# Sums of weight blocks made by ScalarE copies and accumulating transfers instead of VectorE additions, with a new order of the first three steps

## The chip, the cores and the metric

The kernel runs on one core of one Trainium2 chip. A core has a matrix engine (TensorE, PE in the profile, with its weight loads shown as PEld), an element-wise engine for tensor operations (VectorE, DVE), one for activations and copies (ScalarE, ACT), a general engine (GpSimd, POOL) and a fifth one that issues transfers (SyncE, SP). Each engine works through its own list of instructions in order and waits on semaphores for the others. Transfers are carried out by 16 DMA engines and are issued from SP, ACT or POOL. The metric is the time of one execution on the device in microseconds (us); less is better. All times below are in us.

## The reference

The computation is a gated linear attention followed by a two-layer network. Everything is in 32-bit floating point on the chip, with batch 4, 8 heads, 768 tokens and head dimension 48.

```python
f = 1.0 / (1.0 + np.exp(-f_logit))
for t in range(S):
    state = f[:, :, t, :, None] * state + np.einsum('bhd,bhe->bhde', k[:, :, t], v[:, :, t])
    y[:, :, t] = np.einsum('bhd,bhde->bhe', q[:, :, t], state)
x = y.transpose(0, 2, 1, 3).reshape(B * S, H * D)          # 3072 x 384
h = x @ w_in                                               # 384 x 2048
g = np.maximum(h, 0.0) + alpha * np.minimum(h, 0.0)
out = g @ w_out                                            # 2048 x 384
```

The weights w_in and w_out arrive as 64-bit numbers and are turned into 32-bit ones on the chip.

## The kernel before

**Steps.** The 768 tokens of a sequence are cut into 6 chunks of 128, and the 4 batches into 2 pairs. A step is one chunk of one pair, so there are 12 steps (0 to 11, even steps for the first pair, odd ones for the second) of 256 tokens each. In every step the attention of a chunk runs first, then the network on its 256 tokens; the attention of the next steps is woven between the network products of the present one.

**The attention of a step.** The gates f, queries q and keys k are loaded with the head dimension on the partitions (`loaded`, L311 to L323; from SP in step 0, from POOL in all others). ScalarE takes the sigmoid of f (L329) and prepares copies (L330, L331); VectorE builds products of neighbouring gates (`lagged_all`, L338 to L345), running sums (`scanned_all`, L373, L374) and the scaled queries and keys (L380 to L406; in the opening steps also `near`, L641). TensorE makes the score products raw (L582), qu (L591, and L681 in the opening steps) and off (L566, blocks off the diagonal). VectorE copies the scores under masks into `ad` (L599, L451, L702), ScalarE places them in the score matrix A (L606, L573, L688). TensorE multiplies A with the values and the old state (py, L614), ScalarE copies that out as y (L494, L729). For the state, the keys are turned: by TensorE (pk, L713) in the opening steps 0 and 1, through two transfers by DRAM (`turned`, `ksn`) in all others; TensorE multiplies them with the values (pd, L539), VectorE and ScalarE update the state (L550, L554, L556).

**The way into the network.** y has the head dimension on its partitions; the network wants all 384 features of a token there. In step 0 TensorE does this with a placing product (xt, L738) and ScalarE copies the result to xT (L747). In step 1 and in the last step four transfers do it (`by_token`, L626, xT<-y), in the others transfers by DRAM (L503, L505, xT<-tokens).

**The network.** The first layer is eight groups of products (`whole`, L831, tile ph), each with 256 columns of w_in (a "piece" of w_in). ScalarE writes relu(-h) (L854), VectorE combines it with h and alpha (L859), which gives the tile gate. From step 3 on, four of the eight pieces (3 to 6) are split in a high and a low part, with reduced-precision products of hi by xh, lo by xl and a third pass of the sums hi + lo with xs (L831 each time). xl and xs of each step are made by a ScalarE copy and an accumulating transfer from POOL (L820, L823). The parts of w_in are made once: hi by ScalarE (`high_of_w_in`, word Y, L770), lo and the sum by two VectorE operations (`rest_of_w_in`, word Z, L774 and L775). Three sums lie at first in the places of xh, xl and xs; before step 3 the network word T (`turnover`, L796) moves and scales them to their own place, which becomes free when the early tiles are closed.

The second layer of step 0 is plain (po, L866, 32 products of 128 x 384). From step 1 on it is done by a scheme of seven block products of half width (`product`, L886: pa, pc, pb, pa, pd, pe, pf) in place of eight. For it w_out is taken as four blocks b11, b12, b21, b22, and four combinations of them are needed: t3 = b22 - b12, t2 = t3 + b11, t4 = t2 - b21 and t1, the difference of b12 and b11, which replaces b12. In before these are eight VectorE operations (`sum_of_w_out`, words W0 to W7, L809, two halves for each). The gate blocks get four similar sums in every step (L880, words Nm, Nu, Nv, Nw), and the block products are combined at the end of each step (L896, words Nd to Nl).

**The weights' loading.** SP loads 8 pieces of each weight as raw 64-bit words (`load_weights`, L277) into five buffers. For each piece ScalarE makes two passes (L281, L282: words a0 to a7 for w_in, b0 to b7 for w_out), and VectorE adds the two results up (L291: words w0 to w7 for w_in, v0 to v7 for w_out).

**The order.** `ORDER_WORDS` is a list of some two thousand words, written out. `0r1` is part r1 of step 0, `3Na2` is network group a2 of step 3, `W3` is one of the words without a step. Each word calls one part of the program, which issues all its instructions for all engines. A manual schedule keeps this order on PE, DVE and ACT; on POOL and SP a scheduler places the transfers.

**Idle products.** Before the first data arrive, and in gaps of steps 0 and 1, TensorE executes products of ones into an unused bank (`idled`, L935): IDLE = 14 at the start, the words I0 to I5 (BEFORE = 6) up to off of step 0, and J0 to J7 (BEHIND = 8) after it. Their results are not used.

Of the kernel before, what the change touches and what calls it, by code (L numbers as in the profile page):

```python
# [27 lines left out]
IDLE, BEFORE, BEHIND = 14, 6, 8  # L28
# [18 lines left out]
0Np5 W0 1Y1 1X W1 Y3 W2 0Np6 W3 2G 1Na0 W4 W5 0Np7 0No0 2h 1M 0No1 2i 1Nr0 1Na1 Y4 Y5 1Na3 2p 1Nr1 2q W6 1Na2 1Na4
Y6 3e 1Nr2 2u0 2l 1Nc0 1Nr3 2t 1Nc1 2k 1Nm0 1Nr4 1Nc2 2r0 1Nc3 W7 1Nm1 1Na5 1Nc4 1Na6 1Nr5 2R0 1Nr6 2r1 2U0 2K Z3
2u1 1Nc6 2R1 2A0 1Na7 1Nr7 1Nc5 2o 1Np0 2U1 2O 3f 1Nc7 2d Z4 1Nk 2D 2A1 1Np2 3F 1Np1 2y0 2y1 1Np3 2Y0 2Y1 2X 1Nu0
1Nu1 1Nv0 3G 3g 1Np4 1Nd 1Nv1 1Nw0 1Ng 2M 1Nw1 1Ne 1Nj 1Nh 1Np5 3h 1Np6 1Nf 1Nl 3p 1Ni 3i 1NL 2Na0 3l 4e 2Nr0 2Na1  # L50
2Nr1 2Na3 2Na2 1Ns1 3q 2Nr2 3r0 3u0 2Nc0 2Nr3 3k 3t 2Nc1 2Nm0 3R0 3U0 2Na5 2Nc2 2Nc3 2Nm1 2Na4 Z5 2Nr4 3r1 2Nr5 3K
3u1 2Na7 3R1 2Na6 3o 3A0 2Nc5 2Nr6 2Nc4 3O 3U1 2Nc6 Z6 3A1 3d 3D 2Np0 2Nr7 2Np1 2Nk 2Nc7 4f 2Nd T 3y0 3y1 4F 3Y0
2Np2 1Ns0 3Y1 3M 4g 2Np3 4r0 2Nu1 2Nu0 2Np4 3X 2Nv0 4G 2Nv1 2Nw0 2Ng 3Nx 3Ny 2Nw1 2Ne 2Nj 2Nh 2Np5 4h 2Np6 2Nf 2Nl
4p 3Na1 3Nz 3Na0 4i 3Nr0 2NL 2Ni 4k 4l 3NY 3Na2 4q 3Nr1 3Na7 4K 3Na3 5e 2Ns1 3Nr2 3Nc0 3NZ 3Na4 3Nc2 4t 3Nc1 3Nr7
3Nm0 4u0 3Nc7 4R0 4U0 3Nq3 3Na6 4r1 4A0 4R1 3Na5 4u1 4U1 3Nq4 3Nq5 3Nq6 4o 4O 3Nb3 3Nr3 3Nc3 3Nb4 3Nm1 2Ns0 3Nb6
3Nb5 4d 3Nr4 3Nr5 4D 3Np0 4A1 3Nr6 3Nc6 3Nc5 4y0 3Nc4 4y1 3Np2 5f 4M 4Y0 4Y1 3Np1 3Nk 5F 4X 5g 3Np3 3Nu0 3Nu1 3Nv0
5G 3Nv1 3Nw0 3Ng 3Np4 4Nx 4Ny 3Nw1 3Nd 3Ne 5h 3Nj 3Np5 3Np6 3Nh 3Nf 3Nl 5p 3Ni 5r0 4Nz 4Na0 5i 4Nr0 4Na1 3NL 5k 4NY
4Na5 5l 4Nq5 4Na2 5q 4Nr1 5K 4Na3 4Nc0 4Nr2 5u0 5t 4Nc1 4Nm0 4Nc2 5R0 5U0 4Na7 4Nr7 4NZ 4Na4 6e 3Ns1 5r1 4Nc7 4Nq4
4Nq3 5A0 5u1 5R1 5U1 4Na6 4Nb5 4Nb3 5o 4Nq6 4Nr3 5d 5O 4Nc3 4Nb4 5A1 4Nm1 5D 4Nr4 4Nr5 4Nb6 4Np0 4Nr6 5y0 4Nc4 4Nc5
6f 4Nc6 5y1 5Y0 6F 4Np2 5Y1 5X 6g 4Nk 4Np1 4Np3 4Nu0 4Nu1 4Nv0 4Nv1 4Ng 6G 5Nx 5M 4Nw0 4Np4 5Ny 4Nw1 4Nd 3Ns0 4Ne 6h  # L60
4Nj 4Nh 4Np5 4Nf 4Nl 6p 4Ni 5Nz 5Na0 4Np6 6i 5NY 6k 5Nr0 5Na1 4NL 6l 5Na2 6q 5Na7 5Nr1 6t 5Nc1 6u0 5Nr2 5Nc0 6r0
5Nm0 5Nc2 6R0 5Nr7 5NZ 7e 4Ns1 5Na4 6K 5Na3 6U0 5Nc7 5Na5 6r1 5Nq3 6A0 6u1 6R1 6U1 5Nq4 5Nb3 5Nq5 5Na6 5Nb4 6o 5Nr3
5Nq6 5Nc3 6O 6A1 6d 5Nm1 5Nb6 6D 5Nb5 5Nr4 5Nr5 5Np0 5Nr6 5Nc4 5Nc6 7f 6y0 5Nc5 5Nk 7F 6y1 6Y0 5Np2 6Y1 5Np1 6X 7g
5Np3 5Nu0 5Ng 7G 5Nu1 5Nv0 5Nv1 5Nw1 5Np4 6Nx 5Nw0 5Nd 6M 5Ne 6Ny 7h 5Nj 5Nh 5Np5 5Nf 5Np6 4Ns0 7p 5Ni 6Nz 6Na0 5Nl
7i 7l 6NY 6Nr0 6Na1 5NL 7k 7q 6Na2 6Nr1 7t 6Nc1 6Nr2 6Nc0 6Na7 6Nm0 7K 6Na3 6Nq3 7r0 6Nc2 7u0 7R0 6Nr7 6NZ 6Na4 8e
5Ns1 7U0 6Nc7 6Nq4 6Na5 7u1 7r1 6Nq5 7A0 7R1 7U1 6Na6 6Nq6 6Nb3 6Nr3 6Nc3 6Nb4 6Nm1 6Nb6 6Nb5 7A1 7o 6Nr4 6Nr5 6Nc4
6Nr6 7d 8f 6Np0 7O 6Nc5 7D 6Nk 6Np1 7y0 8F 7y1 6Nc6 7Y0 6Np2 7Y1 7X 8g 7Nx 7M 6Np3 6Nu0 6Nu1 6Np4 6Nv0 6Nd 6Nv1 6Nw0
6Ng 8G 7Ny 6Ne 6Nj 6Nw1 8h 6Nh 6Np5 6Nf 7NY 6Np6 5Ns0 6Nl 8p 6Ni 8i 7Nz 7Na0 7Nr0 7Na1 7Nr1 6NL 8k 8l 7Na2 8t 8r0
7Nr2 7Nc0 8q 7Nc1 8R0 9e 6Ns1 8K 7Na3 7Nm0 7Na7 8u0 7Nc2 7Nr7 7NZ 7Na4 8U0 7Na5 7Nq3 7Nq4 7Nc7 8r1 8u1 7Nq5 8A0 7Na6
8R1 7Nb4 7Nb3 8U1 7Nq6 7Nr3 7Nc3 7Nm1 7Nb6 7Nb5 8o 8A1 8d 7Nr4 7Nr5 7Nc4 7Nr6 8D 8O 9f 7Np0 7Nc5 7Nk 7Np1 7Nc6 8y0  # L70
9F 8y1 8Y0 8Y1 7Np2 8X 9g 7Nd 8M 7Np3 7Nu0 7Nu1 8Nx 7Ne 7Np4 7Nv1 7Ng 9G 8Ny 7Nv0 7Nw0 7Nw1 7Np5 7Nh 9h 7Nf 7Nj 9r0
7Np6 6Ns0 7Nl 9p 7Ni 9R0 8Nz 8Na0 8Na7 9i 8Nr0 8Na1 7NL 9k 9l 8Na2 9q 8Nr1 8NY 8Nr2 9t 8Nc0 8Nc2 8Nc1 8Nr7 8NZ 8Na4
10e 7Ns1 8Nm0 9u0 9U0 9K 8Na3 8Na5 8Nq4 9A0 8Nq3 9u1 9r1 8Na6 8Nc7 9R1 9U1 8Nq5 8Nq6 8Nb3 8Nb4 8Nr3 8Nc3 8Nm1 8Nb6
8Nb5 8Nr5 9o 8Nr4 8Nc5 9A1 8Nr6 9O 9d 8Np0 8Nc4 9D 8Nk 8Np1 8Nc6 10f 9y0 9y1 8Np2 10F 9Y0 9Y1 9X 10g 9M 8Np3 8Nu0
8Nu1 10r0 8Np4 8Nd 9Nx 8Nv0 8Nv1 8Nw0 8Ng 10G 8Np5 8Ne 8Nw1 9Nz 10h 9Ny 8Nh 8Nj 8Nf 10p 8Np6 7Ns0 8Nl 8Ni 9NY 9Na0
# [25 lines left out]
def kernel(  # L101
# [845 lines left out]
    with tc.manual_schedule(engines={mybir.EngineType.PE, mybir.EngineType.DVE, mybir.EngineType.Activation}):  # L947
# [10 lines left out]
        for key in ORDER:  # L958
            run[key]()
# [55 lines left out]
```

## Time and profile before

| What | us |
|---|---|
| Time, median of 3 runs | 595.74 |
| lowest and highest of them | 594.69, 597.52 |
| Span of the profiled execution (no other time is given for it) | 592.1 |
| Busy in that span: PE | 580.1 |
| PEld | 527.9 |
| DVE | 505.7 |
| ACT | 300.4 |
| POOL | 68.4 |
| First network product (ph of step 0) starts at | 42.70 |

The time of a run is taken from outside the program, the span from the first to the last event of the profiled execution. The profile gives for each engine its busy time, for slices of the span the share that was busy and the clock granted to TensorE (PEclk, 1.00 is full speed), for each wait who ended it, and for each group of instructions its line, its operation, the shape of its tiles and the mean duration. "A<-B" means that an instruction writes tile A and reads tile B. Where an engine's idle time is given "<-issue", nothing that the profile shows had to be waited for.

The row `0.00:42.70` of the stages below is the opening (the loads and the attention of step 0), `42.70:91.00` is the network of step 0 with the attention of step 1, `91.00:141.00` and `141.00:209.00` hold the networks of steps 1 and 2, and from there on the steps repeat in the same form.

### The profile page before, as it was taken

The numbers are of one execution on the slowest core, as the hardware profiler recorded it, in microseconds if no ns is written. First come the engines' busy times: TensorE is split into PE (matmuls) and PEld (weight loads), VectorE is DVE, ScalarE is ACT, GpSimd is POOL, SyncE is SP. The second block draws the span as 40 slices with busy tenths as digits, with TensorE's granted clock in tenths as the row PEclk, the third lists the DMA queues.
The fourth block names the chain that finished last, engine by engine and source line by source line (L and its number), as shares of the span: only waits on it lengthen the run. The fifth ranks groups of instructions, "written<-read, shape, count | busy, mean of one in ns | idle before, by whom it ended". The sixth has DMA issues, their size and how long they took to land.

```text
span 592.1 us, 18853 instructions
## 1 busy us (share of the span) xinstructions
PE 580.1 (98%) x8200; PEld 527.9 (89%) x8200; DVE 505.7 (85%) x1027; ACT 300.4 (51%) x561; POOL 68.4 (12%) x114
## 2 busy tenths in 40 slices
PE   8799999999999999999999999999999999999997
PEld 6678767899899999999999999899899999899997
DVE  7889799899999989899989889989989979966243
ACT  5697973461472473483382374374275355443230
POOL 9110010000101101111111101101100100100100
PEclk9689999999999999999999999999999999999999
DMA  9959212612523823724624614722732731611300
GB/s 299 356 160 348 98 22 63 172 30 86 123 86 91 191 78 89 172 65 105 169 60 106 153 68 106 164 74 85 148 110 81 152 110 54 112 44 30 80 2 27
DMA packets 69443, 67.57 MB, mean 114 GB/s; under 512 B 44688, under 2 KB 58640, under 8 KB 69360
## 3 DMA queue, kind: packets, MB, share of 16 engines
q1 hardware_dynamic: 59744, 37.16, 22.1%
q0 software_dynamic: 8880, 28.84, 19.2%
q8 instruction: 64, 1.05, 0.7%
q10 hardware_dynamic: 736, 0.37, 0.2%
q14 instruction: 19, 0.16, 0.1%
HBM read 44.99 MB, written 13.50 MB: 99 GB/s over the span
## 4 chain that ended last, share of the span: by engine, by line
PE 80%; issue 10%; DMA 4%; ACT 3%; DVE 3%; POOL 1%; POOLq 0%; ACTq 0%; DVEq 0%
PE ph L831 36%; PE pa L886 9%; PE pd L886 5%; PE pf L886 5%; PE pe L886 5%; PE pb L886 5%; PE pc L886 4%; PE py L614 3%; PE qu L591 3%; PE raw L582 3%; DMA w_out_raw<-in_w_out 2%; PE pd L539 1%; PE off L566 1%; DVE ad L451 1%; DMA f<-in_fT 1%
## 5 line engine op out<-in xcount | busy, mean ns | idle before, releaser
L831 PE MATMUL ph<-xT,w_in_sb 128*128 128x256 f32 x612 | 137.1, 380 | 0.2 <-DMA xT<-y 0.2
L831 PEld LDWEIGHTS ph<-xT,w_in_sb 128*128 128x128 f32 x612 | 115.1, 190 | 16.9 <-issue 0.9
L854 ACT ACTIVATE gate<-ph 128x512 f32<-128x512 f32 x96 | 54.6, 594 | 134.4 <-PE ph L831 127.5
L859 DVE SCALAR_TENSOR_TENSOR gate<-gate,om,ph 128x256 f32<-128x256 f32 x192 | 81.0, 476 | 25.6 <-ACT gate L854 25.1
L886 PE MATMUL pa<-w_out_sb,gate 128*128 128x192 f32 x352 | 61.7, 329 | 0.0
L880 DVE TENSOR_TENSOR gate<-gate 128x512 f32<-128x512 f32 x88 | 57.6, 690 | 3.2 <-PE pb L886 2.4
L886 PEld LDWEIGHTS pa<-w_out_sb,gate 128*128 128x128 f32 x352 | 57.1, 190 | 0.5
L599 DVE COPY_PREDICATED ad<-mraw,raw 128x256 f32<-128x256 int32 (+1 forms) x96 | 42.7, 445 | 8.9 <-PE raw L582 6.2
L451 DVE COPY_PREDICATED ad<-mquad,qu 128x224 f32<-128x224 int32 (+6 forms) x140 | 42.2, 302 | 6.8 <-PE qu L591 1.7
L606 ACT COPY A<-ad 32x256 f32<-32x256 f32 x96 | 38.7, 403 | 11.8 <-DVE ad L451 10.4
L440 DVE TENSOR_TENSOR scores<-scores,fs 128x768 f32<-128x768 f32 (+5 forms) x60 | 37.4, 623 | 1.6
L844 ACT ACTIVATE ph<-ph 128x512 f32<-128x512 f32 x36 | 20.2, 574 | 34.0 <-PE ph L831 25.2
L831 PE MATMUL ph<-xh,hi 128*128 128x256 f32 x216 | 34.4, 295 | 0.0
L831 PE MATMUL ph<-xl,lo 128*128 128x256 f32 x216 | 32.0, 283 | 0.3 <-issue 0.3
L886 PE MATMUL pb<-t,gate 128*128 128x192 f32 x176 | 31.2, 331 | 0.0
L831 PEld LDWEIGHTS ph<-xh,hi 128*128 128x128 f32 x216 | 28.7, 190 | 2.8 <-issue 1.6
L424 ACT COPY A<-q 48x512 f32<-48x512 f32 x44 | 27.2, 617 | 7.8 <-DVE q L398 7.2
L886 PE MATMUL pd<-t,gate 128*128 128x192 f32 x176 | 30.7, 328 | 0.3 <-DVE gate L880 0.3
L886 PE MATMUL pc<-t,gate 128*128 128x192 f32 x176 | 30.6, 327 | 0.0
L886 PE MATMUL pf<-w_out_sb,gate 128*128 128x192 f32 x176 | 30.5, 327 | 0.0
L323 POOL DMA_DIRECT2D vs<-in_v x22 | 13.2, 605 | 149.4 <-PE py L614 149.1
L886 PE MATMUL pe<-w_out_sb,gate 128*128 128x192 f32 x176 | 30.4, 326 | 0.0
(153 smaller groups left out, 1044.0 us busy)
## 6 DMA issues: line engine op xcount, KB each, us to landing
w_out_raw<-in_w_out SPq DMA_DIRECT2D x8, 767.8 KB, 9.6
w_in_raw<-in_w_in SPq DMA_DIRECT2D x8, 767.2 KB, 9.5
q<-in_qT POOLq DMA_DIRECT2D x11, 512.0 KB, 5.1
f<-in_fT POOLq DMA_DIRECT2D x11, 512.0 KB, 5.2
k<-in_kT POOLq DMA_DIRECT2D x11, 512.0 KB, 4.2
turned<-f SPq DMA_DIRECT2D x40, 128.0 KB, 4.4
ksn<-turned SPq DMA_DIRECT2D x10, 512.0 KB, 3.5
out<-o SPq DMA_DIRECT2D x24, 192.0 KB, 1.9
```

What stands on the lines that cost most here:

```text
L424: nc.scalar.copy(A[halves(cc)[1], :, par * HP:(par + 1) * HP, CH * cc:CH * (cc + 1)], x["q3"][rows(par)].rearrange("p (u h c) s t -> p u h ...
L440: nc.vector.tensor_tensor(by_four(us[:, :, UO[m]:UO[m] + 4 * n]), by_four(us[:, :, skip:skip + 4 * n]), spread(fq[:, :, 1:1 + n], n), ALU. ...
L451: nc.vector.copy_predicated(ad[:, u, :, :, 4 * m:DB], mquad[:, lo:lo + n].bitcast(I32).unsqueeze(1).unsqueeze(1).broadcast_to((128, 2, HP, ...
L582: nc.tensor.matmul(raw[DB * j:DB * (j + 1), par, hp * C:hp * C + QW], lhsT=x["k"][r_, g * DB:(g + 1) * DB], rhs=qd[r_, g], start=True, sto ...
L599: nc.vector.copy_predicated(adu[:, :, :, d:4], mraw[:, d, :, d:4].bitcast(I32).unsqueeze(1).broadcast_to((128, H, NB, n)), rv[:, :, QO[d]: ...
L606: nc.scalar.copy(A[s_, u, :, s_], ad[s_, u].rearrange("p r h t -> p (r h) t"))
L831: nc.tensor.matmul(banks[f][:, j * T:(j + 1) * T], lhsT=of[:, kt, 128 * j:128 * (j + 1)], rhs=by[:, kt], start=first_ and kt + j == 0, sto ...
L844: nc.scalar.activation(banks[f], banks[f], AF.Copy, scale=1.0 - 1.0 / EPS)
L854: nc.scalar.activation(to, of, AF.Relu, scale=-1.0)
L859: nc.vector.scalar_tensor_tensor(to[:, j], to[:, j], om[:, m:m + 1], of[:, j], ALU.mult, ALU.add)
L880: nc.vector.tensor_tensor(block(to)[:, p], block(x_)[:, p], block(y_)[:, p], op)
L886: nc.tensor.matmul(banks[to][:, 0:DH], lhsT=block(of)[:, f], rhs=of_w_out(by)[:, f], start=start and f == 0, stop=f == NH - 1, skip_group_ ...
```

## The change

There are four edits.

1. **W: combinations of w_out.** Each of the eight words is now a ScalarE copy of one block (with sign) into the target, then a transfer from POOL that adds the other block to it. t3 = -b12 and then + b22; t2 = b11 + t3; t4 = -b21 + t2; t1 now has the other sign, b11 - b12, so the combinations that use pe (parts f and l of a step's output) have the scale -UP.
2. **Z: parts of w_in.** Each of the four words is a ScalarE copy hi/EPS into lo, a transfer that adds the piece of w_in to it, a ScalarE copy -hi into the sum, and a transfer that adds lo to it.
3. **The words are cut.** A part is now a generator, and a word in the order is one instruction (or a short run of them); a word that stands several times in `ORDER_WORDS` is carried on each time. The loads of a step are four words (ef, eq, ek, ev) in place of one. The manual schedule now covers POOL and SP also, so that their order is written out as well. The tiles that a part makes are made when first needed (`Later`, `ahead`).
4. **The order.** In steps 0 to 2 the order is new on all engines; from step 3 on the order on each engine is that of before, except for the place of the f and q loads on POOL (f, q, k in place of q, f, k where they stand together). BEFORE is 12 in place of 6: six more idle products, I6 to I11.

In numbers of instructions issued: TensorE has 6 more (4434 to 4440), VectorE 16 fewer (1029 to 1013), ScalarE 16 more (573 to 589), POOL 16 more transfers (119 to 135, 384 KB each), SP the same 132. On SP the opening is now f, q, k of step 0, five pieces of w_in (6, 0, 2, 4, 3), the first values, then w_out piece 1 among the rest of w_in, and the other pieces of w_out.

```diff
-IDLE, BEFORE, BEHIND = 14, 6, 8
+IDLE, BEFORE, BEHIND = 14, 12, 8
...
-0e 1e 0I0 0f 0F 0G 0g 0r1 0h 0i 0m 0p 0j 0r0 0I1 0l 0I2 a0 0R0 0I3 0I4 0I5 0q 0o a1 0k a2 0O 0s 0t w0 0u0 0U0 0R1
...
+0ef 0f 0F 0eq 0f 0f 0F 0F 0F 0F 0g 0g 0g 0g 0ek 0F 0g 0I0 0r1 0r0 0I1 a6 0i 0g 0G a0 1ef a2 a0 0G a4 0R0 0h 0j a3 0m
+0R0 0s 1eq 0p 0I2 a6 0I3 0p 0p 0p 0R0 0q a2 a2 0I4 0I5 0R0 0I6 a6 0p 0I7 0s 0I8 a4 0ev 0q 0l 0l 0I9 0I10 0ev a0 0t 0t
+0I11 0o 0O 0O 0u0 0O 0U0 0U0 0U0 0O 0R1 0H0 0H0 0H0 0R1 b1 0k 0K0 0R1 0R1 0K1 0A0 1f w2 0J0 0J1 0A0 0J2 1ek 0H0 0u1
...
+class Later(dict):
+
+    def __init__(self):
+        self.make = {}
+
+    def __missing__(self, key):
+        self[key] = self.make[key]()
+        return self[key]
+
+
+class Word:
+
+    def __init__(self, part):
+        self.part, self.left = part, None
+
+    def __call__(self):
+        if self.left is None:
+            got = self.part()
+            self.left = got if hasattr(got, "gi_frame") else iter(())
+        next(self.left, None)
...
+        def f_():
+            x["kt"] = load("f", fT)
+            x["f"] = quads(x["kt"])
+
+        def q_():
+            x["q"] = load("q", qT)
...
+        return {"ef": f_, "eq": q_, "ek": k_, "ev": v_}
...
+    def added(to, of):
+        nc.gpsimd.dma_start(out=to, in_=of, accum_op=ALU.add)
+
     def rest_of_w_in(f):
-        w, hi = piece_of_w_in(f), late["hi"][:, f - SPLIT[0]].bitcast(F32)
-        nc.vector.scalar_tensor_tensor(late["lo"][:, f - SPLIT[0]], hi, 1.0 / EPS, w, ALU.mult, ALU.add)
-        nc.vector.scalar_tensor_tensor(sums[f - SPLIT[0]], hi, 1.0 / EPS - 1.0, w, ALU.mult, ALU.add)
+        hi, lo = (late[n][:, f - SPLIT[0]] for n in ("hi", "lo"))
+        nc.scalar.activation(lo, hi.bitcast(F32), AF.Copy, scale=1.0 / EPS)
+        yield
+        added(lo.bitcast(F32), piece_of_w_in(f))
+        yield
+        nc.scalar.activation(sums[f - SPLIT[0]], hi.bitcast(F32), AF.Copy, scale=-1.0)
+        yield
+        added(sums[f - SPLIT[0]].bitcast(F32), lo.bitcast(F32))
...
     def sum_of_w_out(n):
-        to, x_, y_, op = (("t3", b22, b12, ALU.subtract), ("t2", "t3", b11, ALU.add), ("t4", "t2", b21, ALU.subtract),
-                          ("t1", b12, b11, ALU.subtract))[n // 2]
+        to, of, sign, more = (("t3", b12, -1.0, b22), ("t2", b11, 1.0, "t3"), ("t4", b21, -1.0, "t2"), (b12, b12, -1.0, b11))[n // 2]
         p = slice(n % 2 * NH // 2, (n % 2 + 1) * NH // 2)
-        to, x_, y_ = (of_w_out(t) if isinstance(t, str) else t for t in (to, x_, y_))
-        nc.vector.tensor_tensor(to[:, p], x_[:, p], y_[:, p], op)
+        to, more = (late[t] if isinstance(t, str) else t for t in (to, more))
+        nc.scalar.activation(to[:, p], of[:, p], AF.Copy, scale=sign)
+        yield
+        added(to[:, p], more[:, p])
...
             if by_parts(f):
                 products(f, late["hi"][:, f - SPLIT[0]], late["xh"], True, False)
+                yield
                 products(f, late["lo"][:, f - SPLIT[0]], late["xl"], False, False)
...
-            f=lambda: plus(side("11"), "pe", side("11")),
+            f=lambda: plus(side("11"), "pe", side("11"), -UP),
...
-            l=lambda: plus(side("01"), "pe", side("01")),
+            l=lambda: plus(side("01"), "pe", side("01"), -UP),
...
-    with tc.manual_schedule(engines={mybir.EngineType.PE, mybir.EngineType.DVE, mybir.EngineType.Activation}):
+    with tc.manual_schedule(engines={mybir.EngineType.PE, mybir.EngineType.DVE, mybir.EngineType.Activation,
+                                     mybir.EngineType.Pool, mybir.EngineType.SP}):
...
+        run = {key: Word(part) for key, part in run.items()}
         for key in ORDER:
             run[key]()
```

More of the change, by code (lines that the diff above doesn't have):

```diff
@@ L47 @@
[L47 to L51, printed above, removed]
@@ L597, in lags @@
         for d in range(4):
+            if d:
+                yield
             n = 4 - d
@@ L633, in opening @@
         i = f"{bp}_{c}"
+        ahead(bp, c, x)
         def two(name):
```

260 lines of the change are left out of this document (171 added, 89 removed).

## The prediction

> **What bounds the kernel now.** I read the page's busy shares, the slices and the chain first, then the five stages, TensorE's waits, the microseconds in which its clock fell, its rows in time, and what the moved work costs. All times are us.
>
> ```profile
> PE 580.1 (98%) x8200; PEld 527.9 (89%) x8200; DVE 505.7 (85%) x1027; ACT 300.4 (51%) x561; POOL 68.4 (12%) x114
> PEclk9689999999999999999999999999999999999999
> PE 80%; issue 10%; DMA 4%; ACT 3%; DVE 3%; POOL 1%; POOLq 0%; ACTq 0%; DVEq 0%
> ```
> ```profile
> 0.00:42.70 42.70, 35.84 (x696) 29.00 (x697) 34.10 (x62) 30.81 (x59) 17.88 (x45) 0.84 0.84 279
> 42.70:91.00 48.30, 48.11 (x518) 36.27 (x513) 44.13 (x76) 39.68 (x69) 3.67 (x6) 1.00 0.44 157
> 91.00:141.00 50.00, 49.95 (x666) 44.32 (x667) 46.15 (x92) 21.40 (x41) 3.40 (x5) 1.00 0.31 86
> 141.00:209.00 68.00, 67.31 (x1054) 60.89 (x1054) 64.13 (x136) 31.97 (x59) 7.43 (x10) 1.00 0.47 118
> 209.00:592.10 383.10, 378.92 (x5297) 357.40 (x5282) 317.16 (x665) 176.58 (x334) 35.97 (x48) 1.00 0.38 93
> ```
> Columns of the stages: window, length, busy time of PE, PEld, DVE, ACT and POOL, TensorE's granted clock, DMA share, GB/s. From 42.70, the first network product, TensorE is busy to within 0.2 a stage (141 to 209: 0.7). Only the first 42.70 hold time that can be won: what TensorE does there is partly filler, and the clock averages 0.84.
>
> ```profile
> PE off_0a L566 <- DVE kh L402: 2.8, 1, 2.8
> PE py L614 <- ACT ad L688: 0.8, 1, 0.8
> PE off L566 <- issue: 0.7, 1, 0.7
> PE pd L886 <- DVE gate L880: 0.3, 1, 0.3
> ```
> ```profile
> 18.00:19.00 1.00, 0.46 (x28) 0.38 (x15) 0.98 (x3) 0.68 (x3) 0.00 (x0) 0.97 1.06 395
> 19.00:20.00 1.00, 1.00 (x7) 1.00 (x6) 0.92 (x3) 0.58 (x2) 0.00 (x0) 0.50 1.02 381
> 32.00:33.00 1.00, 1.00 (x4) 0.80 (x4) 1.00 (x3) 0.96 (x3) 0.00 (x0) 0.70 0.82 328
> ```
> ```profile
> 12.22 2.43 PE L935 MATMUL idle<-ones 128*128 128x256 f32 x10
> 17.47 0.21 PE L566 MATMUL off_0a<-q,kh 48*32 48x32 f32 x1 [2.83 <-DVE kh L402]
> ...
> 42.70 3.50 PE L831 MATMUL ph<-xT,w_in_sb 128*128 128x256 f32 x15
> ```
> The last filler ends at 14.65, TensorE waits 2.83, does small products, and its clock halves at about 19 until 32.6: qu (L591, L681) takes 1.05+1.97 a half where it takes 0.82+1.11 at full clock (65.37, 66.12). After 42.70 VectorE costs TensorE 0.3, so taking work off VectorE (44.13 busy of 48.30) saves by itself almost nothing.
>
> **The change, part by part.**
>
> *VectorE's relief.* Eight W additions (L809, 0.95 each, 0.87 apart) between 79.3 and 107.6 and eight Z (L774, L775, the same) between 113.5 and 168.6 go: 16 x 0.87 = 13.9. Their cover is TensorE, so I enter 0; the bounds are 0 and the 0.3 wait.
>
> *ScalarE's copies.* 16 more copies of 128x768. Nearest row: hi (L770), 0.84, 13.4 in all. ScalarE is busy 21.40 of 50 from 91 to 141, so 0 beside TensorE; without that room, the gates queued behind each copy would be 0.84 late.
>
> *Accumulating transfers.* 16 of 384 KB on POOL. The nearest rows are the same transfer for x:
>
> ```profile
> xl<-xT POOLq DMA_DIRECT2D x9, 384.0 KB, 4.0
> xs<-xl POOLq DMA_DIRECT2D x9, 384.0 KB, 4.0
> f<-in_fT POOLq DMA_DIRECT2D x11, 512.0 KB, 5.2
> w_out_raw<-in_w_out SPq DMA_DIRECT2D x8, 767.8 KB, 9.6
> ```
> They land in 3.9 to 5.6 and cost POOL about 0.9 to issue (16 x 0.9 = 14.4 of a queue busy 12%). The sums are a chain: t3, then t2 from t3, then t4 from t2, each a copy (0.84) and a landing (4.0). A Z is likewise copy, transfer, copy, transfer. Walked in the new order (each instruction after its producers and its queue, with the durations here), t3 is issued at 80.1 and 95.7 (the second behind a load on POOL), t2 lands by 108.6, t4 by 113.5; pb, the first that reads t4, starts about 122.8. The slack of 9 hides it: cost 0. Uncovered, three links at 5.6 instead of 4.0 would add 4.8, still inside. The Z sums land about 165; their reader T (L796) comes about 172. [...]
>
> *The opening's order and six fillers.* A filler is two records, and ten took 2.43, so one is 0.49 at most. Eleven now stand before off, from about 12.2, and end at 17.1 to 17.5. They cost nothing: off (0.69) and then qu follow, and qu waits for VectorE's running products (near, L641) until 19.2 in any case; if VectorE were 1 earlier, they would hold TensorE up by nothing still. Its longest pause falls from 2.83 to under 1.9, so I take the clock to stay full. Then, in the new order: qu of half 0 19.2 to 21.2; pk 1.04, to 22.4; fillers; qu of half 1 23.8 to 25.7; its masked copies (L702, three, 0.91) end 26.65, before 30.24. ScalarE, whose weight passes (0.80 each) are packed earlier, places the blocks by 31.85; y of half 0 32.4, py of half 1 34.0 to 35.1, xt to 37.2, xT copies 38.2. VectorE's two last weight pieces (L291, 0.94) are ready at 38.2 and 39.1, raw of the next step ends 38.9. The first ph starts at 38.9 instead of 42.70: **+3.8**. On the queues: POOL loads f before k and q instead of q first, and SP puts five w_in pieces ahead of v and w_out; the DMA share is 1.0 until 32 either way, so this only chooses which piece is late, and the walk has each at its place in line. If the clock halves all the same, 4.3 after the last filler as before (at 21.5), qu of half 1 ends 28.5 and all is 2.0 to 2.8 later: +1.0 to +1.8. [...]
>
> *From 39 to 91.* Products stay back to back where weights and gates allow; the nearest misses are ph3 (needs VectorE at 47.2, starts 49.3) and ph1 (52.8, 53.6). One load suffers: w_out piece 4 is issued on SP only after ScalarE has freed its buffer at about 60.6, and ScalarE reads it at 66.25. The eight w_out loads took 6.8 to 15.0; off the opening's crowd the 6.8 is nearest, and ScalarE stalls 1.2 with y of the step behind it. So 60.6 + 6.8 - 66.25 = 1.2; the bounds are 0 (buffer free earlier) and 3.9 (9.6). I enter **-1.2**.
>
> *Step 1's network start.* In before, ph waits 0.19 for xT at 90.91 and its first group lasts 3.14 for 2.60. The raw products of step 2 (two of 0.85) now stand in front and cover it: 0.19 + 0.5 = **+0.7**; bounds 0 and 0.7.
>
> *f of step 3.* Its load (L313, POOL) is now issued behind the transposes of step 2, near 95, lands near 100.1 (5.2), and its sigmoid stands at the head of ScalarE's queue from about 98.2 with two gates behind. In before it was issued at 110.03 and read at 120.55. TensorE has 0.9 of slack at that point; I find it short by 0.9 at the sixth ph and take **-0.5**; bounds 0 and -0.9.
>
> *208.* The 0.69 pause before off (no releaser named) disappears since increments now stand in front: **+0.7**; bounds 0 and 0.7. From step 3 on each engine's order is otherwise the same, so 209 to 592 (378.92 busy of 383.10) is entered as 0.
>
> Sum: 3.8 - 1.2 + 0.7 - 0.5 + 0.7 = 3.5. The profile shows only the execution's span, 592.1, with no time of its own beside it; the median of the timed runs, 595.74, lies 3.64 above, and I leave that as it is: 592.1 - 3.5 = 588.6 of span, **592.2** of time, 0.6% less. About 0.5% (2.98) is what a measurement of this kernel can tell from no change.
>
> **The rivals.**
>
> *The clock halves anyway.* For it: before, it fell 4.3 after the last filler although 0.46 to 0.53 of two microseconds were busy. Against: the pause is now shorter. Sum: 1.4 in place of 3.8 gives 1.1, so 594.6 (593.8 to 595.5), the same within the bound.
>
> *Step 3's f is late; the other side.* ScalarE's queue is in order, so a late f stops the gates, and every ph bank behind them. At 100.1 it costs 0.5; the other terms add to 4.0, so it eats the gain when it lands at 103.6 and makes the kernel slower by 0.5% from 106.6. For it: f loads took up to 7.8 and w_out loads 15.0, and the load stands on POOL behind an accumulating transfer. Against: the DMA share is 0.31 there. A landing of 15.0 comes at 110, 10.4 against 4.0: 602.1. I take the middle of this and no change, 599.0 (landed at 106.9).
>
> *No stall from w_out piece 4 nor f.* 3.8 + 0.7 + 0.7 = 5.2: 590.5.
>
> *The sums come late.* Decides when the three links take more than 9 longer, 7 each instead of 4. At 9.6 each, the landing of the weight loads, pb waits 16.8 - 9 = 7.8: 600.1. Against: the x rows, none over 5.6.
>
> **How the numbers follow.** Chances: forecast 0.40 (own range 590.9 to 593.4), clock 0.24, late f 0.16, no stall 0.12, late sums 0.04, others 0.04. Faster: three quarters of the forecast, 0.30, all of no stall, 0.12, and 0.02 = 0.44. Slower: late f 0.15, late sums 0.04, others 0.02 = 0.21. Same: the rest, 0.35. The range runs from 589.6, below the no-stall case, to 599.0, the middle of late f, leaving out about 0.08 of late f, 0.04 of late sums and 0.04 below.
>
> **What will show it.** First ph near 38.9; granted clock 1.00 from 15 to 33, or 0.5 from about 21.5; second half's masked copies ended at 26.7; no wait for xT at step 1; a ScalarE wait of about 1 on w_out's raw words near 66; f of step 3 issued near 95; accumulates landing in about 4; no pause near 208. I am wrong if TensorE gains waits between 39 and 209 that I found covered, or if the steps from 209 on, whose order is the same, come out at another length.

## The result, and the profile after

The changed kernel is slower: 603.74 to 606.65 us in three runs against 594.69 to 597.52 in four, ratio 1.0152 (95% interval 1.0118 to 1.0185). Forecast were 592.2 and a range from 589.6 to 599.0. A fourth run, of 612.87 at a lower granted clock (0.971 against 0.983 to 0.986), is left out of the ratio, and since the first profile shows that run, the lines below come from a second one, of an execution of 605.83 with a span of 604.1.

From the page of the changed kernel (busy times, TensorE's granted clock in 40 slices, and the queue that the page calls instruction):

```profile
PE 587.2 (97%) x8212; PEld 534.5 (88%) x8212; DVE 488.9 (81%) x1011; ACT 312.5 (52%) x577; POOL 83.9 (14%) x130
PEclk9879899989999999999999979999999999999999
q8 instruction: 65, 1.06, 0.7%
```

The change does what it says: VectorE is busy 16.8 us less, ScalarE 12.1 and POOL 15.5 more. But the clock now falls at four places. The same kernel in stages (columns as in the prediction; the cuts are its first network product, first po, and the first pa of steps 1, 5 and 7):

```profile
0.00:42.80 42.80, 36.56 (x709) 29.80 (x709) 31.66 (x57) 30.81 (x57) 14.65 (x41) 0.88 0.80 270
42.80:71.70 28.90, 28.18 (x331) 24.24 (x330) 25.75 (x50) 24.01 (x38) 3.24 (x5) 0.94 0.76 239
71.70:127.80 56.10, 53.31 (x674) 39.45 (x673) 44.48 (x90) 40.03 (x74) 15.09 (x17) 0.94 0.62 129
127.80:310.40 182.60, 182.12 (x2698) 170.21 (x2697) 157.00 (x335) 90.33 (x169) 25.39 (x33) 1.00 0.51 124
310.40:405.80 95.40, 92.87 (x1362) 87.38 (x1360) 82.80 (x173) 45.57 (x86) 10.46 (x14) 0.96 0.43 107
405.80:604.10 198.30, 194.15 (x2459) 183.42 (x2448) 147.17 (x309) 81.74 (x157) 15.10 (x20) 1.00 0.31 77
```

A stage's length splits into three: TensorE idle (length less busy), time lost to the clock (busy time times one less the granted clock, summed over single microseconds), and what is left, the work at full clock.

| Stage, before / after | length | idle | lost to the clock | work |
|---|---|---|---|---|
| to the first network product | 42.7 / 42.8 | 6.9 / 6.2 | 6.8 / 3.9 | 29.0 / 32.6 |
| to the first po | 26.2 / 28.9 | 0.0 / 0.7 | 0.0 / 1.7 | 26.2 / 26.5 |
| to pa of step 1 | 50.2 / 56.1 | 0.2 / 2.8 | 0.0 / 2.9 | 50.0 / 50.4 |
| to pa of step 5 | 184.4 / 182.6 | 0.7 / 0.5 | 0.0 / 0.0 | 183.7 / 182.1 |
| to pa of step 7 | 90.9 / 95.4 | 0.4 / 2.5 | 0.0 / 2.9 | 90.6 / 89.9 |
| to the end | 197.7 / 198.3 | 3.8 / 4.2 | 0.0 / 0.0 | 193.9 / 194.2 |

Outside the opening, work differs by 1.6 at most. The 12.0 us between these two spans are 4.9 more idle time, 4.7 more lost to the clock and 2.4 more work (the six fillers alone would be 2.9, at the 0.49 each of the prediction). So the opening gained nothing, and each of three pauses later (0.72, 2.51 and 2.53) was paid twice: once as a pause, once as a slow stretch behind it. TensorE's waits and the rows behind the longest ones:

```profile
PE raw L681 <- issue: 2.8, 2, 2.5
PE inc L633 <- issue: 2.7, 2, 2.4
PE ph L952 <- DVE gate L983: 2.5, 1, 2.5
PE qu L690 <- issue: 1.0, 2, 0.7
```
```profile
30.91 0.41 PE L633 MATMUL inc<-vs,ksn 64*48 64x48 f32 x7 [2.36 <-issue]
...
65.96 0.39 PE L690 MATMUL qu<-scores,k 48*32 48x52 f32 x25 [0.72 <-issue]
...
119.69 5.46 PE L952 MATMUL ph<-xT,w_in_sb 128*128 128x256 f32 x12 [2.51 <-DVE gate L983]
...
351.67 0.48 PE L681 MATMUL raw<-qd,k 48*32 48x80 f32 x4 [2.53 <-issue]
```

Three of the four end on no releaser at all, in the middle of a burst of small products. Single microseconds around the last of them show the second payment, 0.50 of the clock for almost seven:

```profile
349.00:350.00 1.00, 0.14 (x10) 0.00 (x0) 0.00 (x0) 0.80 (x3) 0.00 (x0) 1.00 0.70 274
350.00:351.00 1.00, 0.00 (x0) 0.00 (x0) 0.00 (x0) 0.00 (x0) 0.00 (x0) 0.87 0.05 20
351.00:352.00 1.00, 0.33 (x4) 0.19 (x4) 0.00 (x0) 0.00 (x0) 0.00 (x0) 0.50 0.00 0
...
357.00:358.00 1.00, 1.00 (x8) 1.00 (x8) 0.96 (x3) 0.98 (x3) 0.00 (x0) 0.72 0.00 0
```

### The profile page after: what moved, and what is told of

Same layout as the page of the kernel before. It is cut to its first block, busy times and chain, and to the rows that moved or that the text cites. A ratio compares the mean times of both kernels' runs of the same rounds, so it can differ in the third digit from the quotient of the medians.

```text
span 611.0 us, 18904 instructions
## 1 busy us (share of the span) xinstructions
PE 591.0 (97%) x8212; PEld 537.4 (88%) x8212; DVE 488.7 (80%) x1011; ACT 312.7 (51%) x577; POOL 84.1 (14%) x130
## 3 DMA queue, kind: packets, MB, share of 16 engines
q8 instruction: 65, 1.06, 0.7%
## 4 chain that ended last, share of the span: by engine, by line
PE 86%; DVE 7%; issue 2%; DMA 2%; ACT 2%; DVEq 0%; ACTq 0%
PE ph L952 37%; PE pa L1010 9%; PE pd L1010 5%; PE pf L1010 5%; PE pe L1010 5%; PE pb L1010 4%; PE pc L1010 4%; PE py L717 4%; PE po L990 3%; PE qu L690 3%; PE raw L681 3%; PE inc L633 2%; DMA q<-in_qT 1%; DVE ad L700 1%; PE off L663 1%
## 5 line engine op out<-in xcount | busy, mean ns | idle before, releaser
L952 PE MATMUL ph<-xT,w_in_sb 128*128 128x256 f32 x612 | 144.9, 394 | 2.5 <-DVE gate L983 2.5
L952 PEld LDWEIGHTS ph<-xT,w_in_sb 128*128 128x128 f32 x612 | 119.1, 197 | 19.9 <-issue 2.8
L983 DVE SCALAR_TENSOR_TENSOR gate<-gate,om,ph 128x256 f32<-128x256 f32 x192 | 82.6, 476 | 33.6 <-ACT gate L976 33.0
L700 DVE COPY_PREDICATED ad<-mraw,raw 128x128 f32<-128x128 int32 (+3 forms) x96 | 42.1, 444 | 14.2 <-PE raw L681 12.2
L407 DVE TENSOR_TENSOR qd<-qd,f 128x768 f32<-128x768 f32 (+2 forms) x36 | 27.1, 754 | 7.6 <-ACT qd L400 7.6
L952 PE MATMUL ph<-xs,sum 128*128 128x256 f32 x216 | 30.7, 293 | 0.0
```

The costliest lines, as they stand in the source:

```text
L407: nc.vector.tensor_tensor(qdv[d], qdv[d - 1][:, :, :, 1:5 - d], f[:, :, 1:5 - d].rearrange("p (g i) r -> p g i r", i=NB), ALU.mult)
L700: nc.vector.copy_predicated(adu[:, :, :, d:4], mraw[:, d, :, d:4].bitcast(I32).unsqueeze(1).broadcast_to((128, H, NB, n)), rv[:, :, QO[d]: ...
L952: nc.tensor.matmul(banks[f][:, j * T:(j + 1) * T], lhsT=of[:, kt, 128 * j:128 * (j + 1)], rhs=by[:, kt], start=first_ and kt + j == 0, sto ...
L983: nc.vector.scalar_tensor_tensor(to[:, j], to[:, j], om[:, m:m + 1], of[:, j], ALU.mult, ALU.add)
```

## The experiments

**The parts one by one.** The new order with W and Z on VectorE, the old order with W and Z by copies and transfers, and the six fillers taken from the new order or added to the old one.

```diff
-        nc.scalar.activation(to[:, p], of[:, p], AF.Copy, scale=sign)
-        yield
-        added(to[:, p], more[:, p])
+        yield
+        if sign > 0:
+            nc.vector.tensor_tensor(to[:, p], more[:, p], of[:, p], ALU.add)
+        else:
+            nc.vector.tensor_tensor(to[:, p], more[:, p], of[:, p], ALU.subtract)
```

The first (Z in the same way, two scalar_tensor_tensor at the places of its transfers):

> The new order with W and Z done by VectorE again, at the places where the changed kernel issues the transfers. Order theory (the new order of steps 0 to 2 costs the 9 us): as slow as the changed kernel, 603 to 606. Transfer theory (16 accumulating transfers crowd the DMA engines and POOL's queue, so that f, q and k of step 3 come late): 594 to 597. Code theory (TensorE's instructions arrive in pieces of 128 matmul records, and it pauses where the next piece is late): the pauses without a releaser stay at the same counts of records, but may change in length.

Measured: 612.6, ratio to before 1.0265 (1.0226 to 1.0305). Slower than the changed kernel by about 7 (1.0265 against 1.0152), which no theory had. In the new order the 16 additions stand among VectorE's gates and masked copies, and TensorE now waits for VectorE and ScalarE in steps 1 and 2 (from the waits between 70 and 230 us):

```profile
PE ph L952 <- ACT A L512: 1.7, 1, 1.7
PE pb L1010 <- DVE gate L983: 1.7, 2, 1.3
PE ph L952 <- DVE gate L983: 1.6, 1, 1.6
```

So the relief of VectorE, worth nothing in the old order, is needed by the new one. The second, `before.py` with the changed `sum_of_w_out` and `rest_of_w_in`:

> The old order with W and Z done by ScalarE copies and accumulating transfers. Order theory: like the kernel before, 595 to 597. Transfer theory: 600 to 605, with a gate wait on TensorE between 110 and 130 us. Code theory: pauses at the same record counts as in the kernel before (2887 and so on), longer where transfers run beside them.

Measured: 603.33, ratio 1.0125 (1.0089 to 1.0160). The transfers' edit alone costs nearly as much as the whole change, but not by a gate wait. A W copy now stands between the two y copies of step 1 in ScalarE's queue (first two rows, ScalarE), and xT comes late (last row, TensorE), with the clock down for 3.4 us behind it:

```profile
86.13 0.84 ACT L813 ACTIVATE t<-w_out_sb 128x768 f32<-128x768 f32 x1
86.88 0.57 ACT L729 COPY y<-py 128x512 f32<-128x512 f32 x1
```
```profile
93.63 1.63 PE L836 MATMUL ph<-xT,w_in_sb 128*128 128x256 f32 x3 [2.80 <-DMA xT<-y]
```

The copy explains only a part of the 2.6 by which this wait has grown (0.19 before): the second y is done 0.97 later, and xT's transfers then land in a median of 5.0 instead of 3.9, beside an accumulating transfer that POOL issued at 87.35, ahead of its own two of them. From the first po to pa of step 1 it takes 55.9 instead of 50.2; 2.6 more are lost from there to pa of step 5, where another wait for xT takes 1.8.

The costs of the parts do not add: about 17 and 8 alone, 9 together. The order and the engine that does the sums were fitted to one another. The fillers:

> The changed kernel with six idle products fewer (BEFORE back to 6). By the prediction's step (the six cost nothing and keep the clock): 605 to 608, with the clock falling earlier. Code theory: TensorE's stream is 12 matmul records shorter ahead of everything, so each pause without a releaser comes 12 records later in the stream's work, and the time changes by up to 5 us either way.

Measured: 603.44, ratio 1.0120 (1.0087 to 1.0152), which overlaps that of the changed kernel, and below the 605 to 608 of the prediction's step. The first network product came at 40.2 instead of 42.8, and the pause of 2.36 in inc is gone; later pauses stayed, one of them longer (2.23 near 216 instead of 0.48).

> The kernel before with six more idle products behind I5, where TensorE waited 2.83 us for off. Prediction's step: clock stays full in the opening, first ph up to 2 us earlier, 593 to 595. Code theory: the stream is shifted by 12 records, so the pause at 208 us moves to another instruction and changes length; 593 to 600. If the fall of the clock does not depend on that pause: 595 to 597.

Measured: 597.46, ratio 1.0035 (1.0017 to 1.0053). The fillers do take the wait of 2.83 away (0.19 is left) and put off the clock's fall from 19 to 27, and yet the first network product comes at 44.0 instead of 42.7: the clock falls all the same, and TensorE pauses 1.82 in the increments. The pauses without a releaser are the second result. Kernel before, kernel before with six fillers (12 matmul records more in front):

```profile
208.66 0.69 PE L566 MATMUL off<-q,kh 48*32 48x32 f32 x57 [0.69 <-issue]
...
343.70 0.87 PE L831 MATMUL ph<-xl,lo 128*128 128x256 f32 x5 [0.35 <-issue]
```
```profile
209.68 0.38 PE L591 MATMUL qu<-scores,k 48*32 48x112 f32 x4 [0.56 <-issue]
...
344.88 0.33 PE L582 MATMUL raw<-qd,k 48*32 48x80 f32 x5 [0.92 <-issue]
```

The first pause has moved from 7 records into off to the last 4 of qu ahead of it, the second from 1 record into its half of a group, past the other half's 6, to the last 5 of raw: 11 and 12 records earlier in the work. Counted from the start, nothing has moved; both profiles hold the same number of recorded matmuls up to each pause (the count behind PE's busy time; kernel before, then with the fillers):

```profile
0.00:208.30 208.30, 200.87 (x2887) 170.14 (x2887) 187.87 (x361) 123.77 (x227) 32.38 (x66) 0.97 0.50 151
...
0.00:343.50 343.50, 335.54 (x4915) 297.06 (x4915) 312.58 (x620) 192.76 (x355) 48.06 (x87) 0.98 0.48 136
```
```profile
0.00:209.40 209.40, 202.00 (x2887) 171.07 (x2888) 187.38 (x360) 123.76 (x227) 32.47 (x66) 0.98 0.49 151
...
0.00:344.70 344.70, 336.15 (x4915) 297.34 (x4916) 311.40 (x617) 192.99 (x355) 47.43 (x86) 0.99 0.48 135
```

Between them lie 2028 = 16 x 126.8 records, and from the packet of the instruction queue that ends ahead of the first pause of the kernel before to the one ahead of its second it is 16 packets. In the changed kernel this queue moved 65 packets while TensorE executed 8212 matmuls and as many weight loads, 126 of each per packet. This is the code theory, a reading of these counts: TensorE's instructions arrive in pieces of about 127 matmuls; a piece lasts 27 us in network products (0.217 each), but under 2 us where qu and raw follow each other (128 in 1.68 from 340.57 on in the kernel before), and there the next one is late. In the changed kernel the pauses come after 349, 477, 983, 3012, 4916 and 6437 recorded matmuls: 128, 4 x 126.5, 16 x 126.8, 15 x 126.9 and 12 x 126.8 apart. In its first profile the pauses come after the same counts, and from each to the next it is 1, 4, 16, 15 and 12 packets.

The trace's transfers show a packet at such a pause. The instruction queue in the microsecond in which raw breaks off in the changed kernel (349 to 350):

```profile
q8 instruction: 1, 0.02, 6.8%
```

This one packet of 16 KB (0.02 MB in the row) begins at 349.18, when TensorE has just run out of work, and takes 1.09 (6.8% of the microsecond of 16 DMA engines); TensorE goes on at 351.67, 1.40 after its end. The other five of the six pauses just counted also end 1.25 to 1.42 after the end of such a packet, and the two of the kernel before 1.45 and 1.43. The packets ahead of the two pauses of the kernel before took 0.96 and 0.95, as long as others; what differs from pause to pause is how early they began. Those two began 1.72 and 2.03 before TensorE ran out of work, and the pauses were 0.69 and 0.35, where it was 2.53 with the packet of 349.18.

**The transfers, the loads, and the boundaries.** Four more: a second profile of the changed kernel, the same without its 16 transfers, q loaded ahead of f again, and the boundaries moved by 28 records.

> The changed kernel once more, for a profile without the clock falls that its first profile showed beyond those of the other kernels. Span 601 to 605; all theories expect the same.

Measured: 605.83; these are the lines of the first section.

```diff
     def added(to, of):
-        nc.gpsimd.dma_start(out=to, in_=of, accum_op=ALU.add)
+        pass
```

> The changed kernel with its 16 accumulating transfers left out (the ScalarE copies stay, the second terms of the differences of w_out and of the parts of w_in are missing). Transfer theory (they slow the loads of q and k of step 3 and with them the gates of step 1): q of step 3 lands in about 5 us, the gate wait of 2.5 us and the wait of the increments near 118 us go, 597 to 600. Order theory (the new order alone is the cause): 602 to 605.

Measured: 602.79, ratio 1.0121 (1.0070 to 1.0172), at the lower end of what the order theory forecast, and not told apart from the changed kernel as a whole. In one stage the transfer theory was right in part: from the first po to pa of step 1 it takes 52.1 instead of 56.1; q lands in 5.2, the increments don't wait and the clock stays up, but a gate wait of 1.59 is left. With the transfers, the landing times in that stretch (85 to 130 us, changed kernel) are far from the 4.0 of the prediction:

```profile
t<-t POOLq DMA_DIRECT2D x4, 384.0 KB, 8.5
...
q<-in_qT POOLq DMA_DIRECT2D x1, 512.0 KB, 7.8
k<-in_kT POOLq DMA_DIRECT2D x1, 512.0 KB, 9.7
```

```diff
 ORDER = flat()
+for n in [n for n in range(4, 12) if ORDER.index(("eq", n)) < ORDER.index(("f", n))]:
+    ORDER.remove(("ef", n))
+    ORDER.insert(ORDER.index(("eq", n)) + 1, ("ef", n))
```

> The changed kernel with q loaded ahead of f on POOL again in steps 4 and 6 to 11, as in the kernel before. Code theory with loads (q and f issued in one go hold up the piece of TensorE's instructions that is fetched meanwhile): the pauses near 215 to 220 and 351 to 358 us shrink from 1.6 to 3.3 us to under 1, the clock stays full there, 599 to 602. If the order of the two loads is worth nothing, as the prediction entered it: 603 to 606.

Measured: 603.33, ratio 1.0132 (1.0088 to 1.0175), inside the forecast for no effect; from the changed kernel it can't be told apart by its time. In the profile the pause in raw is 1.80 where it was 2.53, not under 1 as the code theory had it, at the same 4 products before the end, and the clock holds: pa of step 5 to pa of step 7 takes 92.3 instead of 95.4. This pause differs between executions too: with q behind f it took 2.42 to 3.52 in five profiles (the changed kernel's two, and the runs without transfers, with two transfers moved and with step 3's work put back), so 1.80 lies below all of them, but it is one profile. POOL's queue in the kernel before, and then in the changed one without the six fillers, where the boundary stands at the same 5 records of the same group and the pause is 2.18 instead of 0.35:

```profile
329.58 0.74 POOL L313 DMA_DIRECT2D q<-in_qT  x1 [5.54 <-DVE ks L406]
337.74 0.74 POOL L313 DMA_DIRECT2D f<-in_fT  x1 [7.42 <-DVE ad L599]
```
```profile
342.70 0.74 POOL L369 DMA_DIRECT2D f<-in_fT  x1 [12.51 <-DMA turned<-f]
343.43 0.76 POOL L369 DMA_DIRECT2D q<-in_qT  x1
```

q, which could have gone 8 us earlier, stands behind f, and both are in flight when the next piece is due. The piece's own packet takes no longer for it (0.95 to 1.09), it begins later: 6.0 and 6.1 after the packet before it in the two profiles with q behind f, 4.9 with q ahead, 4.6 in the kernel before.

```diff
+    def tiny(to):
+        nc.tensor.matmul(to[:, 0:32], lhsT=ones[:, 0:128], rhs=ones[:, 0:32], start=True, stop=True)
...
+                run.update({(f"S{k}", 0): lambda: tiny(idle) for k in range(14)})
```

> The kernel before with 14 products of 32 columns behind I5, under the wait of 2.83 us there: 28 matmul records more, hardly any work. Code theory, from the measured boundaries (126.8 records apart in the steady steps, a piece there 3.3 us after the one before it was begun): the pauses at 208 and 343 us go, and new ones come ahead of pa of step 2 (1.7 us), in the third passes of step 5 (1.6), in the groups of step 6 (1.1) and in off of the last step (1.6), 6 us against 1.9, with clock falls on top: 599 to 603. If code does not matter: 595 to 597, as the kernel before.

Measured: 597.73, ratio 1.0035 (1.0014 to 1.0056). That is between the two forecasts. The old pauses went and new ones came (1.20 in step 5, 2.07 in raw near 347), but these products were not small: 28 of them took 3.21, and 72 took 11.44 in the next run, in part at half the clock. So this run and the next mix a longer opening with the moved boundaries; both are repeated below with products that are small.

**The two theories on the changed kernel.** The boundaries moved by 72 records (the same products, 36 times), two transfers put ahead of the loads of step 3, and all three together.

> The changed kernel with 36 products of 32 columns among the idle ones ahead of off of step 0: 72 matmul records more in front of everything, nothing else. Code theory: the pauses in inc of step 0 (2.4 us), in qu of step 1 (0.7), in raw near 351 (2.5) and inc near 451 (0.4) go; the new places (raw of step 1's second half 1.8, inc of step 5 1.0, groups of steps 6 and 8 1.4 and 1.6) cost less, and fewer of them pull the clock down: 598 to 602. If TensorE's code is not what it waits for: 604 to 606.

Measured: 612.22, ratio 1.0295 (1.0241 to 1.0350), outside both forecasts; the first network product came at 52.5.

```diff
+for word, times in ((("W0", None), 1), (("W3", None), 2)):
+    for _ in range(times):
+        at = len(ORDER) - 1 - ORDER[::-1].index(word)
+        ORDER.insert(ORDER.index(("ef", 3)), ORDER.pop(at))
```

> The changed kernel with the second half of t3 and the first half of t2 added ahead of the loads of step 3 on POOL, where the DMA engines are nearly idle. Transfer theory (the loads of step 3 land late because they share the DMA engines with the transfers): q lands in under 7 us where it took 8.5, the gate wait near 119 us falls from 2.5 to under 1.5 and the clock stays up there, 600 to 603. If the order alone is the cause: 604 to 606.

Measured: 608.78, ratio 1.0224 (1.0202 to 1.0246), the wrong way. The two transfers now run beside those that turn the keys of step 2, which f's buffer waits for: these land after 5.6 to 7.9 instead of 2.8 to 5.0. f is issued at 107.97 instead of 103.22, ScalarE waits 6.50 for it at the head of its queue, and TensorE's wait grows from 2.51 to 3.99. This is not the whole of the 3.7 by which the span is longer: its stage gives 1.1; 1.1 more is lost in the opening, where nothing was changed (a pause of 3.21 in inc for 2.36), and 1.1 between pa of steps 5 and 7 (3.52 in raw for 2.53). The wait:

```profile
115.04 1.06 ACT L400 ACTIVATE f<-f 128x1024 f32<-128x1024 f32 x1 [6.50 <-DMA f<-in_fT]
```

> Both of these and q ahead of f in steps 4 and 6 to 11. If the two theories hold together: 594 to 599. If either is wrong: over 600.

Measured: 614.69, ratio 1.0326 (1.0293 to 1.0359), the worst of all, with both faults of the two before it.

**Moving boundaries at little work, and the queue.** Now products of 48x32 by 48x32 (72 took 2.46): 36 of them in the changed kernel, 14 or 64 in the kernel before.

```diff
+    def small():
+        for _ in range(64):
+            nc.tensor.matmul(idle[0:32, 0:32], lhsT=ones[0:48, 0:32], rhs=ones[0:48, 0:32], start=True, stop=True)
```

> The kernel before with 64 such small products: 128 records, just one piece of code, 1.4 us of work under the wait of 2.8 us. Code theory: every boundary stands where it stood, or within 2 records of it, so the pauses come in off near 208 and the group near 343 as in the kernel before: 594 to 597. If added products cost by themselves: slower than the run with 14 of them.

Measured: 600.50, ratio 1.0079 (1.0053 to 1.0105). The control holds in the steady part: after 128 more records the pauses stand at the same instructions as in the kernel before (compare its two rows above).

```profile
214.65 0.69 PE L566 MATMUL off<-q,kh 48*32 48x32 f32 x57 [0.93 <-issue]
...
350.89 0.87 PE L831 MATMUL ph<-xl,lo 128*128 128x256 f32 x5 [1.64 <-issue]
```

They are longer (0.93 for 0.69, 1.64 for 0.35), and the time itself was forecast wrong, because the opening is not free: there the DMA share is 0.99 to 1.14 in each microsecond from 16 to 24, while the weights are loading, and a whole piece of small products runs out within 3.6 us (17.60 to 21.2). TensorE pauses 1.17 in them and 2.86 behind them, and the first network product comes at 48.5.

> The kernel before with 14 such small products: 28 records more, 0.3 us of work under a wait of 2.8 us. Code theory: first ph within 1 us of 42.7, the pauses in off near 208 and in the group near 343 gone, new ones ahead of pa of step 2, in step 5 and in raw near 347, together 4 to 6 us: 597 to 601. If the position in the code does not matter: 594 to 596.

Measured: 599.39, ratio 1.0061 (1.0042 to 1.0080). The pauses near 208 and 343 are gone; of the new ones only that in step 5 came (1.27, though the profile names a releaser for it; it ends 1.5 after an instruction packet, as the others do). The cost lies in the opening: moved by 28 records, a boundary meets the products behind qu of step 0, TensorE pauses for 4.34, and the first network product comes at 45.9. So the time lies in the forecast range by luck.

```profile
27.54 2.07 PE L935 MATMUL off_0a<-ones 128*128 128x256 f32 x4 [4.34 <-issue]
```

> The changed kernel with 36 products of 48x32 by 48x32 among the idle ones ahead of off: again 72 matmul records more in front of everything, this time of the small shape whose records take 11 ns, so under 1 us of work. Code theory: opening pause in inc gone and first ph near 40 to 41; pauses in qu near 66 and raw near 351 gone with their clock falls; new ones, as in the run with the 32-column products, in inc of steps 2 and 3 (1.3 and 2.9 us) and near 270 to 320 and 408 (4.6 together): 600 to 604. If the position in the code does not matter: 605 to 606.

Measured: 611.16, ratio 1.0266 (1.0203 to 1.0328), outside both forecasts. In the steps the pauses did as the code theory said: those in inc of step 0, near 66 and in raw near 351 are gone, and from pa of step 5 to pa of step 7 91.3 passes instead of 95.4; the new ones are in inc of steps 2 and 3 (1.03, 2.34), near 270 (2.03, 0.86) and at 406 (0.88). Their sum and their clock falls (4.6 lost from pa of step 1 to pa of step 5, where the changed kernel loses none) are larger than what went, and the opening, where I expected a gain, pauses 3.64 in qu, so that the first network product comes at 46.1. The three shifts dealt the pauses out anew; they did not remove them.

```diff
 ORDER = flat()
+first = ORDER.index(("f", 3))
+last = len(ORDER) - ORDER[::-1].index(("Nc5", 1))
+held = [w for w in ORDER[first:last] if w[1] == 3 and w[0][0] != "e"]
+ORDER[first:last] = [w for w in ORDER[first:last] if w not in held] + held
```

> The changed kernel with the first 20 words of step 3's attention (sigmoid, scaled q and k, running sums, on ScalarE and VectorE) put behind the gates of step 1, as in the kernel before. Queue theory (the gates of step 1 stand behind instructions that wait for f and q of step 3): the gate wait of 2.5 us near 119 and the clock fall behind it go: 598 to 601, unless raw of step 3 comes late in turn. If the transfers alone are the cause: 604 to 606.

Measured: 612.48, ratio 1.0276 (1.0238 to 1.0314). The gate wait near 119 is gone and the clock stays up: from the first po to pa of step 1 50.5 passes instead of 56.1, with all transfers in place. So that wait belongs to the order of ScalarE's and VectorE's queues. But the work that was put back now stands ahead of the second layer's gate sums in VectorE's queue (128 to 140), with the clock down again behind the wait, and the time is outside both forecasts:

```profile
141.39 1.01 PE L1014 MATMUL pd<-t,gate 128*128 128x192 f32 x2 [7.26 <-DVE gate L1008]
```

None of the versions beats the kernel before.

## Why the prediction was wrong, point by point

- **VectorE's relief, ScalarE's copies** (0 each). Right for the old order's bound, wrong as a statement on the change: without the relief the new order costs 7 more. In the old order the copies are not free either, since one of them stands in front of y and its transfer runs beside y's.
- **Accumulating transfers** (0, by a landing of 4.0). The term was mis-sized: six transfers and the loads of step 3 run at once, and they land in 8.5. The 9 us of slack at pb held all the same, TensorE never waited for a sum. What they cost was the landing of q beside them (7.8): without them there are 1.1 less of waits and 2.7 less lost to the clock in that stage. The DMA share was 1.06 to 1.15 in each stretch of 4 us between 108 and 124 us of the first profile, so the DMA engines were full.
- **The opening and the fillers** (+3.8). The first failed step, twice. "They cost nothing" named VectorE's products as the cover and did not see that fillers shift TensorE's code: six of them cost 0.35% in the old order, and without them the new order's first network product came at 40.2 instead of 42.8. And "I take the clock to stay full" failed although no pause was left that was longer than 1 us: the clock fell at 26.5 after two pauses of 0.60 and 0.25, so the length of the longest pause, on which the step rested, does not decide it. The rival "clock halves anyway" forecast +1.0 to +1.8 for that; by the bounds given there that is 594.2 to 595.0, not 593.8 to 595.5; the code pause of 2.36 in inc covers the rest. In the changed kernel the clock fell behind a pause of 0.72 among small products (66), and with q ahead of f it held behind one of 1.80; that a shorter pause keeps the clock up, which the step took for granted, no run shows.
- **w_out piece 4** (-1.2): did not come. ScalarE has no wait for raw words of w_out there; those loads landed in a median of 4.9, below the 6.8 that I took as the least.
- **Step 1's network start** (+0.7): right, no wait for xT is left.
- **f of step 3** (-0.5). The second failed step. The mechanism was right and the size wrong by a factor of more than ten: 2.8 of waits and 2.9 lost to the clock. f landed at 109.1, where I had 100.1 and had put the point from which the kernel gets slower at 106.6, and behind f stood q, on ScalarE the copies that need it, and behind those the gates. It is the rival on the other side, at its own place; I gave it 0.16. The failed number is the issue: I had it near 95, right behind the transposes of step 2, but the load writes the one buffer that the four transfers of the turned keys read. Rows of the changed kernel (SyncE's queue, then POOL's):

```profile
95.46 3.18 SPq L569 DMA_DIRECT2D turned<-f  x4
...
102.85 0.33 SPq L572 DMA_DIRECT2D ksn<-turned  x1
```
```profile
103.22 0.75 POOL L369 DMA_DIRECT2D f<-in_fT  x1 [10.26 <-DVE q L482]
```

The profile names a VectorE operation as the last thing awaited, but f follows the landing of those four (ksn is issued on it) by 0.4 here and by 0.4 in the run with two transfers moved (107.59, 107.97). So 8.2 of the 9.0 are the issue, and 0.6 the flight (5.8 for 5.2).
- **208** (+0.7): the pause stayed (0.48), because it has nothing to do with what precedes off.
- **209 to the end, entered as 0.** The third failed step: 5.5 of idle time and lost clock from pa of step 5 to pa of step 7, where the kernel before has 0.4. Two things dismissed have a part in it: 12 records more in front of everything (0.92 for 0.35 in the old order), and q behind f on POOL (2.18 for 0.35 without the 12 records). With q ahead again 1.80 is left, so the two are not the whole of it. The prediction's reading of TensorE as busy to within 0.2 a stage also leaves out this stage, which was idle for 4.2 before the change.

What stays open is how the 9 us split over the edits: the runs without the fillers, without the transfers and with the loads' old order each read 1 to 2 faster by their ratios (1.0120, 1.0121 and 1.0132 for 1.0152), and none of the three is apart from the changed kernel by its interval. The pause in inc of step 0 took 1.44 to 3.48 in six profiles whose opening is the same code, so one profile does not settle a difference of that size.

## What to carry to other kernels

TensorE was busy to 98% in this kernel, and its pauses without a releaser in the steady steps were of 0.69 and 0.35; six products put in front, to fill a wait, moved them by 11 and 12 records. In such a kernel, look for waits without a releaser inside bursts of small products, and count matmuls between them. Price a pause with the slow clock behind it, which cost 1.7 to 2.9 more in each of the three cases here. Where an order was fitted by hand to the engines' loads, an edit's cost measured on the old order says little of its cost in the new one, so "the same order from here on" has to be read on the transfer queues also.

## What the runs showed of the hardware

- The pauses without a releaser that are counted above (six in the changed kernel, two in the kernel before) stood some 127 matmul records apart or a multiple of it (2028 records and 16 packets of the instruction queue between the two of the kernel before, which moved 64 packets for 8200 matmuls). The packets were of 16 KB and took 0.88 to 1.39 there and 0.88 to 1.55 in the first profile of the changed kernel; after a pause work went on 1.25 to 1.56 after the end of one (both profiles of the changed kernel and the kernel before). In the steady steps such pauses took 0.35 (kernel before, 343) to 3.52 (two transfers moved, raw), and up to 4.34 while the weights were loading (14 small products); with a DMA share of 0.00 to 0.07 from 347 to 350 in the run with q ahead of f one was still 1.80.
- In the changed kernel pauses of 0.7 to 2.5 were followed by a clock of 0.50 for 3.4 or 6.8 us, a loss of 1.7 to 2.9, but not always: with q ahead of f the clock stayed at 1.00 behind 1.80. Nor did each fall have a pause just ahead of it: in the run with 36 products of 32 columns the clock fell at 20.3 with TensorE busy in every microsecond from 14 on. What sets the moment of a fall was not shown.
- At full clock, matmul records of 32 columns took 0.08 to 0.11 each with 128 x 128 weights (12 in each microsecond from 16 to 20, the changed kernel with 36 of these products; 28 in 3.21, the kernel before with 14), and 0.034 with 48 x 32 ones (72 in 2.46, the changed kernel with 36); 32 columns alone did not make them cheap here.
